# Two layers of causal convolution and GeGLU on one core: a new order of chunks and layers, with handover visits in halves

## The chip, the cores and the metric

The kernel runs on one core of one Trainium2 chip. The metric is device time in microseconds (us): the median of 3 runs of the kernel before is 909.96 us (909.64 to 910.38). One execution was profiled; its span is counted from the first to the last instruction of the program.

The core's engines run side by side, each through its own list of instructions in order: PE (matrix products; its weight loads are listed as PEld), DVE and ACT (elementwise work), POOL (small elementwise work and transfers), SP (transfers only). They wait for each other through semaphores. DMA transfers are issued by SP, POOL or ACT and carried out by 16 DMA engines.

## The reference

`x` has 2048 tokens of 576 features (bf16 inputs). Two times over, a convolution layer A and a feed-forward layer B are added to it:

```python
x = A_q
for _ in range(2):
    h = layernorm(x)
    k4 = sum(shift(A_k, 3 - t) * A_shift_k[:, t] for t in range(4))   # causal, 4 taps
    kv = k4 * A_v
    y = causal_conv(kv, A_ssm_k) + kv * A_ssm_D                       # 2048 taps, by FFT
    x = x + h * y
    h = layernorm(x)
    x = x + (gelu(h @ B_w_gate) * (h @ B_w_up)) @ B_w_down            # 576 -> 4608 -> 576
```

`y` doesn't depend on `x`, so one convolution serves both layers.

## The kernel before

**Chunks, units, passes, visits.** The tokens are cut into 4 chunks of 512, each of 4 rows of 128 tokens. A unit is (layer, chunk); units 0 to 7 are (0,0) (0,1) (1,0) (1,1) (0,2) (0,3) (1,2) (1,3). The feed-forward weights don't stay on the chip: a pass streams all of them once, in 3 phases of 12 feature tiles (of 128 features), and serves the units in its list, `passes = [[0], [1, 2], [3, 4], [5, 6], [7]]`. One phase of one unit is a visit; there are 24.

**A visit** (the loop at L1640 and after). For each of 12 feature tiles `gu` (L1099 to L1104) does 18 matmuls of 64x128 weights by 512 tokens, in pairs on the two halves of the array's rows, into one of three PSUM banks in turn; ACT makes the GELU (L1691 or L1700; L1692 copies the other factor too when ACT has time) and DVE the product into `hT` (L1693, L1701), which frees the bank. Then `two_rows` (L1755) does the product with the down weights for rows 0 and 1, then 2 and 3: 48 matmuls of 288 columns a row, in two steps, first half of the array's rows, then the other half. Between the steps stands `hold` (L1135): a NOP on ACT or DVE that waits for the first step and that PE waits for before the second. DVE adds the result to `x_c` (L1798 to L1806).

**The handover chain.** When the last phase of a layer-0 unit ends, each row of its chunk goes: sum into `x_c` with the row's sum (DVE L1798), mean (POOL L933), sum of squares (ACT L941), `rstd` (POOL L948, L949), `yh` = 1 + y * rstd (ACT L977), `x_c` * ... (DVE L987), mean, squares and `rstd` again, normed row `xn` (DVE L1016, L1018), and its transpose into `xnT` by DMA (`spread`, L1055: two DMA transposes from SP, of 5 and of 4 blocks of 128 columns). `xnT` is what the next unit's feature tiles read.

**The convolution** works in 4 blocks of 512 tokens. For block m the spectra of block and filter are made on PE (`fwd`, `fwd_h` for block 1, 8 matmuls at a step; `fwd4` with `quarter` for blocks 2 and 3, 4 matmuls at a step, whose sums and differences DVE finishes), the spectra of all earlier blocks are multiplied on DVE (`prod`), folded, and turned back on PE (`inverse`). This work is spread between the feature tiles.

**What sets the order.** The program is written out instruction by instruction in Python. `Pace` keeps a planned clock of PE, DVE and ACT with costs such as `C_GU` for a feature tile; `fill` (L1165) puts other work behind each tile until a limit. `weights` (L1145) issues weight loads from SP: 3 buffers of gate and up weights (`load_wgu`, L868, three transfers each, 4 feature tiles) and 3 of down weights (`load_wd`, L880). A load waits in SP's queue until PE has left the buffer, and what stands behind it waits too.

Of the kernel before, what the change touches and what calls it, by code (L numbers as in the profile page):

```python
# [24 lines left out]
NP = 3  # L25
# [8 lines left out]
C_P0, C_P1, C_AC = 1.28, 1.35, 0.7  # L34
C_TT, C_ST, C_BN, C_NORM, C_HT, C_GELU, C_EVA, C_EVD, C_YH = 0.74, 0.80, 0.47, 0.62, 0.615, 0.51, 0.56, 0.72, 0.7
C_HB = 0.345
C_FOLD = 0.46
# [3 lines left out]
SLOW, PRESS = 5.0, 22.0  # L41
# [93 lines left out]
class Conv:  # L135
# [9 lines left out]
    def __init__(self, tc, ctx, pace, gwork, xtp, A_k, A_v, A_shift_k, A_ssm_k, A_ssm_D, ident, cps, ypool):  # L145
# [22 lines left out]
        self.nT = self.cst.tile([P, 5, P], BF16, name="nT")  # L168
        self.V_ = self.cst.tile([P, 2, RT, P], BF16, name="V")
        self.nV = self.cst.tile([P, 3, P], BF16, name="nV")  # L170
# [124 lines left out]
    def fwd_eo(self, src, kt, s, h, ring, scale=1.0):  # L295

        nc = self.nc
        ps = yield from self.both_steps(lambda ps: [ps[:, e, 0:HW] for e in range(2)],
                                   [([self.fw(kt, s, i + e) for e in range(2)],
                                     [src(i + e)[:, h * HW:(h + 1) * HW] for e in range(2)]) for i in (0, 2)])  # L300
        eo = self.eo_tile(ring)
        nc.scalar.activation(out=eo[:], in_=ps[:, :, 0:HW], func=ACT.Copy, scale=scale)
        return eo

# [16 lines left out]
    def quarter(self, src, e, s, h, scale=1.0):  # L321
# [5 lines left out]
        eo = self.eop.tile([P, 2, HW], F32, tag="eo", name="eo")  # L327
        nc.scalar.activation(out=eo[:], in_=ps[:, :, 0:HW], func=ACT.Copy, scale=scale)  # L328
        return eo

    def cross(self, eo, lo, hi):
        for dst, op in ((lo, ALU.add), (hi, ALU.subtract)):
            self.nc.vector.tensor_tensor(out=dst, in0=eo[:, 0, :], in1=eo[:, 1, :], op=op)

# [59 lines left out]
    def step(self, m, kv=None, loaded=False):  # L394
# [74 lines left out]
        def fwd(kt, s, h):  # L469
            def run():  # L470
                if s == 0 and h == 0:
                    for k in (kt, kt + 2):
                        kc[k] = self.kcp.tile([P, 2, D], BF16, tag="kc", name="kc")
                free, ring = self.eo_free(True)
                self.eo_at[ring].popleft()
                cur = self.cur
                eo = yield from self.fwd_eo(lambda i: self.vt_[m][:, i, :], kt, s, h, ring)
                done = t.on_act(C_EVA, max(t.pe + 0.25 + LAG, free))
                self.ps_free[cur] = done
                if (kt, s, h) == (1, 1, 1):  # L480
                    self.fwd_at[m] = t.pe + 0.25
                cols = slice(h * HW, (h + 1) * HW)

                def fin():
                    self.cross(eo, kc[kt][:, s, cols], kc[kt + 2][:, s, cols])
                    when = t.on_dve(2 * C_BF, done + LAG)
                    self.eo_at[ring].append(when + LAG)
                    mark(("kc", kt, s, h), when + LAG)
                    if s == 1 and h == 1 and m < self.NB - 1:
                        for k in (kt, kt + 2):  # L490
                            self.spill(self.Kd[m][k], kc[k], when + LAG)
                self.U.append((done + LAG, 2 * C_BF, fin))
            return run

        hh = self.hh if m == 1 else {}

        def fwd_h(kt, s, h):
            def run():
                if (kt, s, h) == (0, 0, 0):
                    self.hh_tiles()  # L500
                free, ring = self.eo_free(True)
                self.eo_at[ring].popleft()
                cur = self.cur
                eo = yield from self.fwd_eo(self.ht[m], kt, s, h, ring, 1.0 / NFQ)
                done = t.on_act(C_EVA, max(t.pe + 0.25 + LAG, free))
                self.ps_free[cur] = done
                if (kt, s, h) == (1, 1, 1):
                    self.hf_at[m] = t.pe + 0.25
                    if loaded:
                        self.hr_free[0] = self.hr_free[1] = self.hf_at[m]  # L510
                cols = slice(h * HW, (h + 1) * HW)

                def fin():
                    self.cross(eo, hh[kt][:, s, cols], hh[kt + 2][:, s, cols])
                    when = t.on_dve(2 * C_BF, done + LAG)
                    self.eo_at[ring].append(when + LAG)
                    mark(("hh", kt, s, h), when + LAG)
                    if s == 1 and h == 1:
                        for k in (kt, kt + 2):
                            self.spill(self.Hd[m][k], hh[k], when + LAG)  # L520
                        if kt == 1:
                            self.hd_at[m] = when + 10.0
                self.U.append((done + LAG, 2 * C_BF, fin))
            return run
# [3 lines left out]
        def v(kt, a, part):  # L528
            def run():
                K = kc[kt] if a == m else kr[(kt, a)][1]  # L530
                if m == 1 and a == 0:
                    prs[part, a, kt] = self.prod(part, K, hh[kt], hr[(kt, a)][1][:, part, :])
                else:
                    prs[part, a, kt] = self.prod(part, K, hr[(kt, a)][1])

                def fin(when):
                    if part == 1:
                        if m == 1:
                            self.hr_free[hr[(kt, a)][0]] = when if a else NEVER
                        else:  # L540
                            self.hr_free[hr[(kt, a)][0]] = when
                        if a < m:
                            self.kr_free[kr[(kt, a)][0]] = when
                return fin
            return run

        def more(kt, part, a):
            def run():
                if a == 1:
                    acc[kt, part] = self.acp.tile([P, D], F32, tag="ac", name="ac")  # L550
                into = acc[kt, part][:]
                nc.vector.tensor_tensor(out=into, in0=prs[part, 0, kt] if a == 1 else into, in1=prs[part, a, kt], op=ALU.add)

                def fin(when):
                    if m == 1 and part == 1:
                        self.hr_free[hr[(kt, 0)][0]] = when
                return fin
            return run
# [40 lines left out]
        for kt in KTS:  # L599
            order = [(a, part) for a in range(m + 1) for part in range(2)]  # L600
            if m == 1:
                order = order[2:]
                for k in (kt, kt + 2) if kt < 2 else ():
                    for part in range(2):
                        self.V.append((get(("ld", k, 0), ("ldk", k), *[("hh", kt, s, h) for s in range(2) for h in range(2)]),
                                       C_P1 if part else C_P0, v(k, 0, part)))
            for a, part in order if kt < 2 else sorted(order, key=lambda k: k[1]):
                keys = [("ld", kt, a)] + ([("kc", kt % 2, s, h) for s in range(2) for h in range(2)] if a == m or m > 1 else [])
                self.V.append((get(*keys), C_P1 if part else C_P0, v(kt, a, part)))
                if a > 0:  # L610
                    self.V.append((now, C_AC, more(kt, part, a)))
                if kt >= 2 and a == m:
                    self.V.append((now, 2 * C_EVD, both(kt, part)))
                    self.V.append((now, 2 * C_TB, shift(kt - 2, part)))
# [5 lines left out]
        def fwd4(filt, e, s, h):  # L620
# [3 lines left out]
            def run():  # L624
                free = self.eo_at["eo"].popleft()
                cur = self.cur
                eo = yield from self.quarter(src, e, s, h, scale)
                done = t.on_act(C_EVA, max(t.pe + 0.13 + LAG, free))
                self.ps_free[cur] = done
                if last:  # L630
                    (self.hf_at if filt else self.fwd_at)[m] = t.pe + 0.13
                cols = slice(h * HW, (h + 1) * HW)

                def first():
# [4 lines left out]
                    else:  # L639
                        if s == 0 and h == 0:  # L640
# [4 lines left out]
                    self.eo_at["eo"].append(t.on_dve(2 * C_BF, done + LAG) + LAG)  # L645

                def second(n):
                    def run():
# [9 lines left out]
                        if n == 1 and last:  # L658
# [7 lines left out]
                            if filt:  # L666
                                self.hd_at[m] = when + 10.0
                    return run
# [1201 lines left out]
```

## Time and profile before

| | us |
|---|---|
| median of 3 runs | 909.96 |
| span of the profiled execution | 907.9 |
| difference | 2.06 |
| PE busy | 902.9 |
| DVE busy | 556.8 |
| ACT busy | 364.5 |
| POOL busy | 142.0 |

The page gives busy time by engine, the span in 40 slices, the chain of work that ended last, and groups of instructions by line with their count and mean duration. A matmul's listed duration reaches from its start to its modelled end, and matmuls overlap; how fast PE goes is read from the starts of successive groups. DMA issues are listed with the time from issue to landing.

### The profile page before, as it was taken

How to read it: one execution, taken by the hardware profiler on the slowest of the kernel's cores; microseconds unless marked ns; L12 is line 12 of the kernel's file. 1: busy time of each engine (PE TensorE's matmuls, PEld its weight loads, DVE VectorE, ACT ScalarE, POOL GpSimd, SP SyncE). 2: the span in 40 equal slices, each digit the busy share in tenths (PEclk: the TensorE clock that was granted, in tenths of full speed). 3: DMA queues.
4: the chain of work that ended last, by engine and by line, in shares of the span. 5: the costliest groups of instructions: out<-in, count | busy, mean ns of one | idle time of the engine just before them, and what ended most of it. 6: DMA issues, size and time to landing. Idle time of an engine off the chain costs nothing.

```text
span 907.9 us, 24267 instructions
## 1 busy us (share of the span) xinstructions
PE 902.9 (99%) x10465; PEld 601.3 (66%) x10465; DVE 556.8 (61%) x1109; ACT 364.5 (40%) x677; POOL 142.0 (16%) x311
## 2 busy tenths in 40 slices
PE   9999999999999999999999999999999999999998
PEld 7757656577576675775766766757757657667666
DVE  8898988654789876667888744553333334433332
ACT  7784446625434356354244233451121224321211
POOL 5423003320113012230023001220000002100000
PEclk9999999999999999999999999999999999999999
DMA  9999967877519503974934702762720820777630
GB/s 242 314 265 285 231 143 137 179 232 135 170 56 258 128 3 67 270 201 102 251 120 123 167 14 69 138 124 63 136 79 3 157 80 14 142 178 179 135 102 28
DMA packets 128272, 129.73 MB, mean 143 GB/s; under 512 B 43298, under 2 KB 120483, under 8 KB 128164
## 3 DMA queue, kind: packets, MB, share of 16 engines
q1 hardware_dynamic: 119138, 93.22, 47.7%
q0 software_dynamic: 8880, 34.36, 11.0%
q8 instruction: 82, 1.34, 0.6%
q10 hardware_dynamic: 146, 0.59, 0.2%
q14 instruction: 26, 0.21, 0.1%
HBM read 106.91 MB, written 11.80 MB: 131 GB/s over the span
## 4 chain that ended last, share of the span: by engine, by line
PE 98%; POOL 0%; ACT 0%; issue 0%; DVE 0%; ACTq 0%
PE gu L1103 61%; PE dn L1768 30%; PE cps L310 2%; PE ps L284 2%; PE dn L1729 1%; PE ps L1344 0%; PE ps L1103 0%; PE ps L1479 0%; POOL rstd L1564 0%; PE ps L1257 0%; PE ps L1315 0%; PE cps L373 0%; PE ps L278 0%; ACT yh L1526 0%; PE ps L1373 0%
## 5 line engine op out<-in xcount | busy, mean ns | idle before, releaser
L1103 PE MATMUL gu<-xnT,wgu 64*128 64x512 bf16 x5148 | 561.4, 376 | 0.0
L1103 PEld LDWEIGHTS <-wgu 64*128 64x128 bf16 x5220 | 293.2, 94 | 260.6 <-issue 0.7
L1768 PE MATMUL dn<-wd,hT 64*128 64x288 bf16 x4512 | 293.9, 283 | 0.0
L1768 PEld LDWEIGHTS <-hT 64*128 64x128 bf16 x4512 | 254.4, 94 | 26.2
L1700 ACT ACTIVATE ga<-gu 128x512 f32<-128x512 f32 x175 | 104.4, 597 | 311.0 <-PE gu L1103 307.8
L1701 DVE TENSOR_TENSOR hT<-ga,gu 128x512 bf16<-128x512 f32 x175 | 120.1, 687 | 167.5 <-ACT ga L1700 167.3
L1691 ACT ACTIVATE ga<-gu 128x512 bf16<-128x512 f32 x111 | 66.2, 597 | 149.9 <-PE gu L1103 143.9
L1693 DVE TENSOR_TENSOR hT<-ga 128x512 bf16<-128x512 bf16 x112 | 47.0, 421 | 59.6 <-ACT ga L1692 59.5
L1692 ACT CAST ga<-gu 128x512 bf16<-128x512 f32 x111 | 64.3, 579 | 0.0
L933 POOL TENSOR_SCALAR means<-s 128x1 f32<-128x1 f32 x28 | 10.4, 372 | 248.7 <-DVE x_c L1798 219.4
L1804 DVE SCALAR_TENSOR_TENSOR x_c<-dn,means,x_c 128x576 f32<-128x576 f32 x28 | 22.8, 815 | 28.4 <-PE dn L1768 28.4
L1806 DVE TENSOR_TENSOR x_c<-x_c,dn 128x576 f32<-128x576 f32 x32 | 24.1, 752 | 25.8 <-PE dn L1768 25.5
L949 POOL TENSOR_TENSOR rstd<-ve,neghalf_t 128x1 f32<-128x1 f32 x56 | 35.4, 632 | 4.7
L345 DVE TENSOR_TENSOR prod<-prod 128x576 bf16<-128x576 bf16 x64 | 29.3, 458 | 2.2
L328 ACT ACTIVATE eo<-cps 128x576 f32<-128x576 f32 x32 | 20.8, 651 | 23.5 <-PE cps L310 17.3
L1785 DVE TENSOR_TENSOR xn<-x_c,dn 128x576 bf16<-128x576 f32 x15 | 11.3, 754 | 26.5 <-PE dn L1768 24.2
L656 DVE TENSOR_TENSOR kc<-ab,cd 128x288 bf16<-128x288 f32 x64 | 25.3, 452 | 0.0
L443 POOL DMA_DIRECT2D kr<-Kd x20 | 11.2, 558 | 88.2 <-DVE prod L344 88.2
L941 ACT ACTIVATE junk<-x_c,nm 128x576 bf16<-128x576 f32 x28 | 21.5, 769 | 2.2 <-POOL nm L933 1.6
L977 ACT ACTIVATE yh<-y,rstd 128x576 f32<-128x576 bf16 x28 | 21.4, 768 | 1.1 <-POOL rstd L949 1.1
L448 POOL DMA_DIRECT2D hr<-Hd x32 | 17.8, 556 | 24.1 <-DVE prod L344 22.6
L948 POOL TENSOR_SCALAR ve<-ss 128x1 f32<-128x1 f32 x56 | 13.9, 248 | 43.7 <-ACT junk L941 43.4
(177 smaller groups left out, 626.4 us busy)
## 6 DMA issues: line engine op xcount, KB each, us to landing
wgu<-in_B_w_gate_dram SPq DMA_DIRECT2D x45, 576.0 KB, 5.9
wd<-in_B_w_down_dram SPq DMA_DIRECT2D x30, 864.0 KB, 7.1
wgu<-in_B_w_up_dram SPq DMA_DIRECT2D x45, 512.0 KB, 7.5
hr<-Hd POOLq DMA_DIRECT2D x32, 288.0 KB, 4.6
kr<-Kd POOLq DMA_DIRECT2D x24, 288.0 KB, 3.9
Kd<-kc POOLq DMA_DIRECT2D x12, 288.0 KB, 6.4
k<-in_A_k_dram POOLq DMA_DIRECT2D x3, 1008.0 KB, 10.3
wgu<-in_B_w_up_dram SPq DMA_DIRECT2D x45, 64.0 KB, 7.3
```

The source lines that it names most:

```text
L345: nc.vector.tensor_tensor(out=dst[:, cols], in0=pr[:, 0, cols], in1=pr[:, 1, cols], op=ALU.subtract if part == 0 else ALU.add)
L656: nc.vector.tensor_tensor(out=into[k][:, plane, cols], in0=a, in1=b, op=op)
L949: nc.gpsimd.tensor_tensor(out=v["rstd"][:], in0=ve[:], in1=neghalf_t[:, 0:1], op=ALU.pow)
L1103: nc.tensor.matmul(cols(pair[:, s, :]), lhsT=w[r0:r0 + HK, k, gi * P:(gi + 1) * P], rhs=cols(xnT[r0:r0 + HK, blk_of[k], :]), start=(k == 0 ...
L1691: nc.scalar.activation(out=ga[:, 0, :], in_=pair[:, 0, :], func=ACT.Gelu_apprx_tanh)
L1692: nc.scalar.copy(out=ga[:, 1, :], in_=pair[:, 1, :])
L1693: nc.vector.tensor_tensor(out=hT[:, fi, :], in0=ga[:, 0, :], in1=ga[:, 1, :], op=ALU.mult)
L1700: nc.scalar.activation(out=ga[:], in_=pair[:, 0, :], func=ACT.Gelu_apprx_tanh)
L1701: nc.vector.tensor_tensor(out=hT[:, fi, :], in0=ga[:], in1=pair[:, 1, :], op=ALU.mult)
L1768: nc.tensor.matmul(acc[:, g, 0:HW], lhsT=lhs[r], rhs=wn[r, g * HW:(g + 1) * HW], start=step == 0 and fi == 0, stop=step == 1 and fi == FP - 1)
L1804: nc.vector.scalar_tensor_tensor(out=xh, in0=acc[:, :, 0:HW], scalar=m_[:, 0:1], in1=xh, op0=op, op1=ALU.add)
L1806: nc.vector.tensor_tensor(out=xh, in0=xh, in1=acc[:, :, 0:HW], op=ALU.add)
```

## The change

1. `passes = [[0], [2], [1], [3, 4], [5, 6], [7]]`: chunk 0 goes through layer 0 and straight through layer 1, then chunk 1. There are 6 passes over the weights in place of 5, still 24 visits.
2. Unit 2 now follows unit 0 and unit 3 follows unit 1 with no visit between. The last visit of units 0 and 1 and the first of units 2 and 3 (`SPLIT`) are done in halves: 12 feature tiles for the 256 tokens of rows 0 and 1, those rows' down products, then the same for rows 2 and 3. So the first half of the next unit needs rows 0 and 1 alone.
3. For units 2 and 3 (`at_once`) a row's 5-block transpose is issued by SP and its 4-block transpose by ACT; rows are normed two at a time.
4. Weight loads in these visits get due times by halves (`pieces`, `size`).
5. Block 1 of the convolution takes the form of blocks 2 and 3 (`fwd4`, `quarter`); products are multiplied first and joined after.
6. Small ones: a scratch row `junk` of its own, `nT` and `nV` in the start's memory, `prep` of chunk 1 later, costs of `Pace` retuned.

```diff
-    passes = [[0], [1, 2], [3, 4], [5, 6], [7]]
+    passes = [[0], [2], [1], [3, 4], [5, 6], [7]]
     NWB = len(passes) * NP
+    at_once = [units.index((1, c)) for c in range(2)]
+    SPLIT = {(units.index((0, c)), NP - 1) for c in range(2)} | {(n, 0) for n in at_once}
...
         tasks = [gate_step(c, j, g, v[j], layer == 1)]
+        if ui in at_once:
+            return tasks + [norm(i) for i in range(j - 1, j + 1) if j % 2]
...
-    def spread(xnT, j, xn):
+    def spread(xnT, j, xn, engs):
         tok = slice(j * P, (j + 1) * P)
         for (b0, nb, c0) in ((0, 5, 0), (5, 4, HK)):
-            nc.sync.dma_start_transpose(out=xnT[:, b0:b0 + nb, tok], in_=xn[:, c0:c0 + nb * P])
+            engs[b0 // 5].dma_start_transpose(out=xnT[:, b0:b0 + nb, tok], in_=xn[:, c0:c0 + nb * P])
...
-            spread(xnT_of[ui], j, xn)
+            if ui in at_once:
+                spread(xnT_of[ui], j, xn, (nc.sync, nc.scalar))
+                t.on_act(C_ISSUE)
+            else:
+                spread(xnT_of[ui], j, xn, (nc.sync, nc.sync))
             xn_done[ui] = j + 1
...
-            if conv_first:
+            if conv_first and not pressing():
...
         def steps(filt, ready):
-            limit = lambda: max(ready(), 0.0 if self.eo_at["eo"] else NEVER)
-            if m > 1:
-                for h in range(2):
-                    for e in range(2):
-                        for s in range(2):
-                            self.Pq.append((limit, 0.25, fwd4(filt, e, s, h)))
-                return
-            for kt in range(2):
-                for s in range(2):
-                    for h in range(2):
-                        self.Pq.append((lambda: max(
-                            ready(), 0.0 if self.eo_at["eo"] or self.eo_at["yh"] else NEVER), 0.49, (fwd_h if filt else fwd)(kt, s, h)))
+            limit = lambda: max(ready(), 0.0 if self.eo_at["eo"] or m == 1 and self.eo_at["yh"] else NEVER)
+            for h in range(2):
+                for e in range(2):
+                    for s in range(2):
+                        self.Pq.append((limit, 0.25, fwd4(filt, e, s, h)))
...
+            split = (ui, ph) in SPLIT
+            def inputs(rows):
+                coming[0], due_at[0] = ui, t.pe
+                while xn_done.get(ui, 0) < rows:
...
+            inputs(RT // 2 if split else RT)
...
+            def features(part=None):
+                last = final and part != 0
+                size = 1.0 if part is None else 0.5
+                cols = (lambda a: a) if part is None else (lambda a: a[:, part * CH // 2:(part + 1) * CH // 2])
+                while late:
+                    add_late()
+                for fi in range(FP):
...
+                        gu(pair, w, gi, cols, xnT)
...
+                    if gi == FG - 1 and last:
+                        group = fi // FG * FG * C_GU
+                        when_due(t.pe + ((FP - FG) * C_GU + 12.0) * size + group * (pieces(at + 1) - size), load_wgu, n + 3)
...
+            for part in range(2) if split else (None,):
+                if part == 1:
+                    inputs(RT)
...
+                features(part)
+                ahead[:] = [t.pe + RT * FP * C_DN, None if split or at + 1 == len(visits) else visits[at + 1][2]]
+                for j in (0, 2) if part is None else (2 * part,):
+                    rows(j)
```

More of the change, by code (lines that the diff above doesn't have):

```diff
@@ L467, in step @@
                            load(kt, a)))
[L469 to L493, printed above, removed]
@@ L495, in step @@
-        hh = self.hh if m == 1 else {}
[L497 to L524, printed above, removed]
@@ new lines, in step, with products, mult, run @@
+        acc = {}
+        halfway = set()
+        def products(kt, items):
+            tiles = {}
+            own = m == 1 and items[0][0] == 0
+            def mult(n):
+                a, part = items[n]
+                def run():
+                    if not tiles:
+                        for i in range(len(items)):
+                            tiles[i] = self.prp.tile([P, 2, D], BF16, tag="prod", name="prod")
+                    K = kc[kt] if a == m else kr[(kt, a)][1]
+                    self.mul(part, K, hh[kt] if own else hr[(kt, a)][1], tiles[n])
+                    def fin(when):
+                        if (kt, a) not in halfway:
+                            halfway.add((kt, a))
+                            return
+                        self.hr_free[hr[(kt, a)][0]] = NEVER if own else when
@@ L542, in fin, with join @@
                         if a < m:
                             self.kr_free[kr[(kt, a)][0]] = when
-                return fin
-            return run
+                    return fin
+                return run
+            def join():
+                for n in reversed(range(len(items))):
+                    a, part = items[n]
+                    dst = hr[(kt, a)][1][:, part, :] if own else tiles[len(items) - 1][:, n, :]
+                    self.join(part, tiles[n], dst)
+                    prs[part, a, kt] = dst
+                return lambda when: None
@@ L547, in more, with ready @@
+            def ready(a):
+                if own:
+                    return get(("ld", kt, 0), ("ldk", kt), *[("hh", kt % 2, s, h) for s in range(2) for h in range(2)])
+                return get(("ld", kt, a), *([("kc", kt % 2, s, h) for s in range(2) for h in range(2)] if a == m or m > 1 else []))
+            steps = [(ready(items[n][0]), C_M1 if items[n][1] else C_M0, mult(n)) for n in reversed(range(len(items)))]
+            return steps, (now, len(items) * C_BF + 0.02, join)
         def more(kt, part, a):
@@ new lines, in ssm_geglu_kernel, with begin @@
+            inputs(RT // 2 if split else RT)
+            if xn_done[ui] < RT:
+                due_at[0] = t.pe + FP * C_GU / 2 + 2 * FP * C_DN
+            else:
+                due_at[0] = t.pe + FP * C_GU + RT * FP * C_DN
+                coming[0] = next((v[2] for v in visits[at + 1:] if v[2] != ui), None)
+            def begin():
+                for kind, n in at_start.get((ui, ph), []):
+                    if kind == "es":
+                        act_early(n)
+                    elif kind == "x":
+                        load_x(n)
+                    else:
+                        for j in range(RT):
+                            vq.extend(prep(n, j))
@@ L1755, in two_rows @@
                 some = math.ceil((gone[-1] + 0.5 - t.pe) * 2 / C_DN) - (FP - 1)
-                some = max(0, min(FP - 3, some)) if j == 0 else 0
+                some = max(0, min(FP - 3, some)) if j == 0 or split else 0
                 order = ([(0, 0, fi) for fi in range(FP - 2)] + [(1, 0, fi) for fi in range(some)] +
```

256 lines of the change are left out of this document (126 added, 130 removed).

## The prediction

> **What bounds the kernel now.** I read the page's busy times and slices first, then the chain of work that ended last, then the stretches.
>
> ```profile
> span 907.9 us, 24267 instructions
> PE 902.9 (99%) x10465; PEld 601.3 (66%) x10465; DVE 556.8 (61%) x1109; ACT 364.5 (40%) x677; POOL 142.0 (16%) x311
> PE 98%; POOL 0%; ACT 0%; issue 0%; DVE 0%; ACTq 0%
> ...
> 446.82 23.31 PE gu L1103 x216
> 470.13 11.76 PE dn L1768 x192
> 481.89 23.31 PE gu L1103 x216
> ...
> 40.00:435.00 395.00, 394.90 (x4640) 259.37 (x4640) 304.22 (x644) 199.27 (x379) 78.12 (x167) 1.00 0.69 170
> ```
>
> PE sets the end: 98% of the chain is PE. A busy PE could hide stalls, so the starts matter: a visit takes 23.31 + 11.76 = 35.07 us, which is 216 matmuls of 512 columns at 107.9 ns and 192 of 288 columns at 61.25 ns, and one visit follows the other without a gap. From 40 to 435 us, where convolution and handovers lie, PE is idle for 0.10 us. So no waiting is there to be won: the change can gain only what it takes out of PE's own work, and any wait that it puts in front of PE is lost in full.
>
> **PE's own work.** Counted in the two kernels' lists of instructions: block 1's spectra fall from 128 matmuls of 288 columns to 64; 864 matmuls of 512 columns become 1728 of 256; nothing else changes on PE.
>
> ```profile
> 40.02 3.12 PE L1103 MATMUL ps<-xnT,wgu 64*128 64x256 bf16 x54
> 42.98 0.41 PE L310 MATMUL cps<-ht,T 64*128 64x288 bf16 x4
> ...
> 44.21 0.65 PE L310 MATMUL cps<-ht,T 64*128 64x288 bf16 x8
> 44.70 2.11 PE L1103 MATMUL gu<-xnT,wgu 64*128 64x512 bf16 x18
> ```
>
> Eight spectra matmuls move the next start by 0.49 us, 61.25 ns each: 64 fewer give -3.9 us. The 54 matmuls of 256 columns take 42.98 - 40.02 = 2.96 us, 54.8 ns each: 1728 x 54.8 - 864 x 107.9 = 94.7 - 93.2 = +1.5 us (0 if they took half of a full one, +4.4 at 56.5 ns, the listed end of that group). Together **-2.4 us** (-3.9 to +0.5).
>
> **The sixth pass over the weights** costs no PE time: slices that moved 230 to 314 GB/s ran with PE at 9 tenths.
>
> ```profile
> PE   9999999999999999999999999999999999999998
> GB/s 242 314 265 285 231 143 137 179 232 135 170 56 258 128 3 67 270 201 102 251 120 123 167 14 69 138 124 63 136 79 3 157 80 14 142 178 179 135 102 28
> ...
> q1 hardware_dynamic: 119138, 93.22, 47.7%
> ```
>
> A single-unit pass of 3 x 35.07 = 105 us moves at most 93.22 / 5 = 18.6 MB (q1 has little but weights), 178 GB/s. In a split visit a weight buffer is released with tile 3 of the second half and wanted again at the half's end, 17.7 - 4 x 0.99 = 13.7 us later, against some 8 us to load it (both below). Each us by which a load outgrew that would be lost in full; I take 0.
>
> **The handovers.** Four times PE now needs two rows' transposes before it may go on: H1 and H2 (rows 0, 1 and rows 2, 3 of unit 2), H3 and H4 (of unit 3). The cover is half a visit: 12 x 18 x 54.8 ns + 96 x 61.25 ns = 11.8 + 5.9 = 17.7 us, in which the whole chain of two rows must run. The prices:
>
> ```profile
> L1700 ACT ACTIVATE ga<-gu 128x512 f32<-128x512 f32 x175 | 104.4, 597 | 311.0 <-PE gu L1103 307.8
> L1692 ACT CAST ga<-gu 128x512 bf16<-128x512 f32 x111 | 64.3, 579 | 0.0
> L941 ACT ACTIVATE junk<-x_c,nm 128x576 bf16<-128x576 f32 x28 | 21.5, 769 | 2.2 <-POOL nm L933 1.6
> L977 ACT ACTIVATE yh<-y,rstd 128x576 f32<-128x576 bf16 x28 | 21.4, 768 | 1.1 <-POOL rstd L949 1.1
> L1693 DVE TENSOR_TENSOR hT<-ga 128x512 bf16<-128x512 bf16 x112 | 47.0, 421 | 59.6 <-ACT ga L1692 59.5
> L1016 DVE TENSOR_SCALAR xn<-x_c,nm,rstd 128x576 bf16<-128x576 f32 x28 | 16.1, 576 | 1.5 <-POOL rstd L949 1.5
> L1018 DVE COPY xn<-xn 128x64 bf16<-128x64 bf16 x28 | 5.1, 182 | 1.0
> L700 ACT ACTIVATE y<-cps 128x576 bf16<-128x576 f32 x12 | 7.6, 655 | 11.0 <-PE cps L310 11.0
> ...
> L1058 SPq DMA_TRANSPOSE xnT<-xn x56: 1200/1257/2270, 142.2 to 786.1; - x56
> DMA to landing us min/median/max: 2.5/2.6/5.2
> ...
> wgu<-in_B_w_up_dram SPq DMA_DIRECT2D x45, 512.0 KB, 7.5
> ...
> 126.10 0.60 SPq L874 DMA_DIRECT2D wgu<-in_B_w_gate_dram  x1
> 126.76 0.63 SPq L875 DMA_DIRECT2D wgu<-in_B_w_up_dram  x1
> 127.44 0.63 SPq L876 DMA_DIRECT2D wgu<-in_B_w_up_dram  x1
> ```
>
> One queue issues a transpose every 1.26 us, each lands 2.6 us after its issue began: four from SP alone would take 3 x 1.26 + 2.6 = 6.4 us. In the changed program the two queues don't run side by side: wherever the queue changes, the transpose waits for the other queue's to have landed. H1 reads ACT row 0, then SP row 0 (waits for it), ACT row 1 (waits), SP row 1 (waits): four landings in a row, 4 x 2.6 = 10.4 us. H2: both of SP, then both of ACT; H3: both of ACT, then both of SP; H4: SP, ACT, ACT, SP.
>
> The Trainium skill ("DMA: Bandwidth & Descriptors", section "Silent corruption: two transposing streams in flight at once") asks for just this: transposes from SP and from ACT are two streams, and the later one's first must wait for the earlier one's full completion count. No run here shows what happens without.
>
> Times from the start of each half, with a 256-column GELU at 0.4 us (an estimate between half of 597 ns and all of it), the copy likewise, and 0.2 us from PE to ACT (the x8 group's listed end, 0.65, is 0.16 us past the next start):
>
> H1. ACT has its first transpose behind GELU and copy of tile 10 of 0 to 11, whose matmuls end at 10.85; ACT also does four sums of squares and two `yh`, 6 x 0.77 = 4.6 us, which by the order of its list pushes it by some 0.3: 12.1. Landings at 14.7, 17.4, 20.1; the fourth can be issued at 20.2. But SP's queue holds three weight transfers between its two transposes (16.1 to 17.9, 1.9 us of issue); the large second one lands 7.5 us after its issue at 16.7, so at 24.2, and the fourth transpose, behind it, at 24.6 (22.8 if it lands alone; 25.4 at the 5.2 us row). Loss 24.6 - 17.7 = **6.9**. Behind ACT's second transpose stands the `hold` NOP for which PE waits between the down steps: PE stops from 15.0 to 18.8 and ends at 21.7, so even early landings leave 4.0.
>
> H2. Four inverse steps (4 full matmuls, 0.49 us each) and a spectrum step (0.25) lengthen the cover to 19.9. Both `xn` stand on DVE behind tile 11's `hT`: 11.8 + 0.2 + 0.4 + 0.4 + 0.2 = 13.0, done at 14.6; SP's second is issued at 15.05 and lands at 17.7, ACT's go at 17.7 and 18.95, landing at 21.6. Behind them on ACT stand a `hold` NOP and a PSUM eviction (0.66 us) that PE needs, from 18.95 + 1.26 = 20.2 to 20.9, and some 20 matmuls of PE's after that (1.3 us): PE ends near 22.2. Loss **2.3** (1.6 to 4).
>
> H3. ACT's second is behind row 1's `xn` (13.9), lands at 16.6; SP goes at 16.7 and 17.95, landing at 20.6, or 21.0 behind the weights issued from 11.9. Loss **3.3** (2.2 to 5). H4. Cover 18.2; landings 14.3, then ACT from 15.6 to 18.2, then 20.9. Loss **2.7** (2 to 4.5). Unit 4, prepared in the second half of unit 3's visit, has its last norm behind ACT's work after tile 11 and lands at 19.3 against 18.4: **0.9** (0 to 2).
>
> Sum of losses 16.1 us, bounds 4.0 + 1.6 + 2.2 + 2.0 = 9.8 and (H1 at 9, two landings at the maximum) 24.5.
>
> **The sum.** 907.9 - 2.4 + 16.1 = 921.6 of span. The median stands 909.96 - 907.9 = 2.06 us above the span, work outside the first and last instruction, unchanged: **923.7 us**.
>
> **The rivals.**
>
> *The queues overlap, or landings come early enough (faster).* Place: the waits between SP's and ACT's transposes. If they cost nothing, the last transposes land at about 15, 18, 17 and 17 us, inside 17.7 to 19.9 us of cover, and only the -2.4 stays: 907.9 - 2.4 + 2.06 = 907.5. It decides where a pair of rows has landed 17.7 us after its half began. Against it stand the waits in the program and 2.6 us as the least that each change of queue costs; for it that both lists leave PE saturated elsewhere. 0.08. With losses of 1 to 4 us left it would be within 0.2% (1.8 us either way, about what a measurement of this kernel can tell from no change): 0.04.
>
> *PE runs slow after the new gaps.* PE has no gap like these before, except at the start:
>
> ```profile
> 3.88 2.20 PE ps L1315 x8
> ...
> 28.05 3.20 PE ps L1479 x26
> ...
> 4.00:7.00 3.00, 3.00 (x20) 1.75 (x19) 2.31 (x4) 2.33 (x5) 0.01 (x1) 1.00 0.96 316
> ```
>
> Of the same 128x288 form, 8 took 275 ns each at 3.88 us, 26 took 123 ns each at 28.05 us, though the granted clock is shown as 1.00. If the first 5 us after a gap run at half rate, a gap costs 2.5 us more. H1 has two gaps of 3 us or more, H3 one, H2 and H4 shorter ones: two gaps hit give 923.7 + 5 = 928.7, all five 936. 0.20. The Trainium skill ("TensorE: Matmul & The Clock Gate", "Part 1: The HAM clock gate") has PE fall to half rate after an idle window of about 3.4 us and stay there for about as long; by that figure a gap costs an estimated 1.7 us, and gaps under the window nothing. No gap of that length stands in this trace.
>
> *Everything at its earliest (less slow).* At the lower bounds 907.9 - 2.4 + 9.8 + 2.06 = 917.4; that is the low end of the forecast's case, not one of its own.
>
> **How the numbers follow.** Forecast, slower through waiting transposes with PE at full rate (916 to 931): 0.68. Slower with a slow PE besides (925 to 936): 0.20. Faster 0.08, same 0.04. So slower 0.88. The range from 915 to 932 leaves out the 0.12 of the faster cases and some 0.08 of the slow-PE case above it.
>
> **What would show it.** In the changed kernel's trace PE should be idle some 16 us in all between about 125 and 420 us, in four places, the largest ahead of unit 2's first tile, each ended by a transpose's landing, or by ACT's NOP behind a transpose. SP and ACT transposes should never be in flight together, each 2.5 us or more after the other. Half tiles should start every 0.99 us. Wrong would be: gaps ended by DVE, POOL or weights; landings well under 2.5 us; PE idle under 5 us; or a total below 912.

## The result, and the profile after

The changed kernel takes **968.54 us** (median of 4 runs, 966.54 to 969.51) where the kernel before takes 909.86 us on the same chip: ratio 1.0642, 95% interval 1.0627 to 1.0657. The forecast was 923.7 us, 915 to 932. The direction was right; the loss is 58.7 us where 13.7 were forecast. The profiled execution took 966.54 us, its span is 964.8 us, 56.9 us longer than before.

The page of the changed kernel, PE's rows, the granted clock, and the shares of the chain that ended last:

```profile
PE 915.9 (95%) x11265; PEld 608.8 (63%) x11265; DVE 568.7 (59%) x1191; ACT 371.3 (38%) x748; POOL 142.6 (15%) x311
PE   9999994999899999677899999999999999999998
PEclk9999997999899999889999999999999999999999
PE 88%; DMA 6%; DVE 3%; issue 1%; ACT 1%; POOL 1%; SPq 0%; ACTq 0%; DVEq 0%; POOLq 0%
```

PE is no longer busy throughout: there is a hole in slice 6 (145 to 169 us), a small one in slice 10 (241 to 265 us) and a long one in slices 16 to 19 (386 to 482 us), and in slices 6, 10, 16 and 17 the clock is below full speed, which it nowhere was before. DMA has come into the chain with 6%. What PE waited for in the changed kernel (us in total, times, longest):

```profile
PE gu L1086 <- DMA xnT<-xn: 21.6, 4, 13.3
PE dn L1775 <- ACTq L1118: 10.0, 3, 8.4
PE gu L1086 <- issue: 4.9, 2, 4.5
PE cps L300 <- ACT eo L318: 2.2, 1, 2.2
PE gu L1086 <- DMA wgu<-in_B_w_up_dram: 2.1, 1, 2.1
PE gu L1086 <- DMA wgu<-in_B_w_gate_dram: 1.7, 1, 1.7
```

The first two lines are the forecast's mechanism: the transposes into `xnT`, and `hold`'s NOP (L1118) that stands behind a transpose in ACT's list. Most of the third, 4.5 us, is the second stop at H1: no releaser is listed, but PE goes on at 166.85 us, 0.09 us after the last transpose landed. The fourth is the first stop at H4, for a PSUM eviction of ACT's (L318, at 434.13 us) that stands behind ACT's two transposes. The last two are weights, which the forecast had at nothing. The chain of waits of the changed kernel through H1 and H3 shows what a transpose took (start, us, what):

```profile
145.15 7.78 DMA xnT<-xn
...
153.07 2.61 DMA xnT<-xn
...
157.01 0.02 ACTq L1118
...
162.34 4.51 issue
166.85 5.15 PE gu L1086 x47
...
396.33 13.55 DMA xnT<-xn
...
411.35 2.59 DMA xnT<-xn
...
414.07 5.97 PE gu L1086 x75
```

The order is the forecast's: ACT, then SP once ACT's has landed, then ACT again. But ACT's took 7.78 us at H1 and 13.55 us at H3 where the forecast had 2.6. SP's list in the changed kernel shows what was in flight: weight loads issued within 4 us ahead of the transposes of 145.15 and 396.33 us.

```profile
141.82 0.59 SPq L853 DMA_DIRECT2D wgu<-in_B_w_gate_dram  x1
142.46 0.64 SPq L854 DMA_DIRECT2D wgu<-in_B_w_up_dram  x1
...
394.51 0.60 SPq L853 DMA_DIRECT2D wgu<-in_B_w_gate_dram  x1
395.31 0.60 SPq L854 DMA_DIRECT2D wgu<-in_B_w_up_dram  x1
```

At H2 nothing else was in flight, and the same four transposes (line L1037 from 180 to 195 us) landed as forecast:

```profile
DMA to landing us min/median/max: 2.4/2.5/2.6
```

Stretches of the changed kernel (us, then the busy time and count of PE, PEld, DVE, ACT, POOL, then the granted clock):

```profile
148.37:157.07 8.70, 0.29 (x6) 0.09 (x1) 2.94 (x7) 0.00 (x0) 0.00 (x0) 0.67 0.70 110
157.07:161.50 4.43, 4.43 (x38) 3.29 (x39) 0.77 (x2) 0.00 (x0) 0.22 (x1) 0.50 1.14 215
162.05:166.85 4.80, 0.29 (x6) 0.03 (x1) 0.77 (x2) 0.00 (x0) 0.21 (x1) 0.80 0.43 64
166.85:171.80 4.95, 4.95 (x48) 4.08 (x50) 0.70 (x2) 1.79 (x5) 0.76 (x2) 0.50 0.55 178
188.00:190.00 2.00, 0.55 (x11) 0.32 (x7) 1.71 (x4) 0.23 (x1) 0.00 (x0) 1.00 0.51 102
252.00:257.00 5.00, 4.97 (x26) 2.03 (x28) 0.00 (x0) 0.92 (x2) 0.00 (x0) 0.50 1.15 214
400.46:414.07 13.61, 0.29 (x6) 0.03 (x1) 0.77 (x2) 0.87 (x2) 1.00 (x4) 0.62 0.83 210
414.07:417.00 2.93, 2.93 (x28) 2.34 (x30) 0.37 (x1) 0.38 (x1) 0.00 (x0) 0.50 0.89 296
436.10:441.80 5.70, 0.37 (x7) 0.16 (x3) 1.55 (x3) 1.66 (x3) 0.22 (x1) 0.97 0.76 77
```

The stretches of 8.70, 4.80, 13.61 and 5.70 us are gaps. The stretches right behind the first three have a clock of 0.50: PE is listed as fully busy and does half the work. So has 252 to 257 us, behind two waits for weights of 1.9 and 2.4 us with one matmul between them. The gap of 1.7 us inside 188 to 190 us leaves the clock at 1.00.

Taking every start of a matmul against the start before it plus that matmul's own time (107.9, 54.8 or 61.25 ns), the 56.9 us are:

| | forecast | measured |
|---|---|---|
| PE's own work | -2.4 | -2.0 |
| H1, idle | 6.9 | 8.6 + 4.7 = 13.4 |
| H2 | 2.3 | 1.7 |
| H3 | 3.3 | 13.5 |
| H4 | 2.7 | 2.5 + 5.6 = 8.0 |
| unit 4 | 0.9 | 2.4 + 1.1 = 3.5 |
| unit 2's third phase (weights) | 0 | 1.9 + 2.4 = 4.3 |
| three more gaps under 1 us each | 0 | 2.0 |
| matmuls at half speed behind six of these places | 0 | 11.2 |
| delays of under half a us | 0 | 1.3 |
| sum | 13.7 | 56.9 |

The weights' stall lies ahead of the visit that starts at 249.5 us; it is unit 2's third phase, though the expectations below call it the second. PE's own work: unit 0's second visit starts at 79.3 us in place of 83.05 (-3.8), and later visits have 1.8 us more.

### The profile page after: what moved, and what is told of

Same layout as the page of the kernel before. It is cut to its first block, busy times and chain, and to the rows that moved or that the text cites. A ratio compares the mean times of both kernels' runs of the same rounds, so it can differ in the third digit from the quotient of the medians.

```text
span 964.8 us, 26089 instructions
## 1 busy us (share of the span) xinstructions
PE 915.9 (95%) x11265; PEld 608.8 (63%) x11265; DVE 568.7 (59%) x1191; ACT 371.3 (38%) x748; POOL 142.6 (15%) x311
## 4 chain that ended last, share of the span: by engine, by line
PE 88%; DMA 6%; DVE 3%; issue 1%; ACT 1%; POOL 1%; SPq 0%; ACTq 0%; DVEq 0%; POOLq 0%
PE gu L1086 58%; PE dn L1775 24%; DMA xnT<-xn 4%; DMA wgu<-in_B_w_up_dram 2%; PE ps L284 1%; PE cps L300 1%; PE dn L1736 1%; DVE x_c L1811 1%; PE ps L1329 0%; DVE kc L636 0%; PE ps L1464 0%; PE ps L1086 0%; DVE prod L331 0%; PE ps L1240 0%; POOL rstd L1548 0%
## 5 line engine op out<-in xcount | busy, mean ns | idle before, releaser
L1086 PE MATMUL gu<-xnT,wgu 64*128 64x512 bf16 (+1 forms) x6012 | 576.9, 349 | 31.8 <-DMA xnT<-xn 21.6
L1086 PEld LDWEIGHTS <-wgu 64*128 64x128 bf16 x6084 | 321.9, 95 | 276.6 <-issue 31.1
L1775 PEld LDWEIGHTS <-hT 64*128 64x128 bf16 x4512 | 239.0, 94 | 55.0 <-issue 11.5
L1708 DVE TENSOR_TENSOR hT<-ga,gu 128x512 bf16<-128x512 f32 (+1 forms) x198 | 122.9, 623 | 196.1 <-ACT ga L1707 195.9
L1707 ACT ACTIVATE ga<-gu 128x512 f32<-128x512 f32 (+1 forms) x198 | 107.7, 545 | 299.3 <-PE gu L1086 297.4
L1698 ACT ACTIVATE ga<-gu 128x512 bf16<-128x512 f32 (+1 forms) x136 | 70.8, 520 | 170.7 <-PE gu L1086 166.3
L1700 DVE TENSOR_TENSOR hT<-ga 128x512 bf16<-128x512 bf16 (+1 forms) x137 | 50.4, 372 | 69.6 <-ACT ga L1699 69.3
L1699 ACT CAST ga<-gu 128x512 bf16<-128x512 f32 (+1 forms) x136 | 68.3, 503 | 0.0
L318 ACT ACTIVATE eo<-cps 128x576 f32<-128x576 f32 x48 | 30.9, 655 | 34.7 <-PE cps L300 28.2
L1792 DVE TENSOR_TENSOR xn<-x_c,dn 128x576 bf16<-128x576 f32 x15 | 11.3, 753 | 23.0 <-PE dn L1775 20.7
L1805 DVE SCALAR_TENSOR_TENSOR x_c<-dn,x_c 128x576 f32<-128x576 f32 x16 | 12.1, 757 | 20.0 <-PE dn L1775 19.2
L323 DVE TENSOR_TENSOR ab<-eo 128x288 f32<-128x288 f32 x48 | 19.3, 451 | 7.7 <-ACT eo L318 4.4
## 6 DMA issues: line engine op xcount, KB each, us to landing
k<-in_A_k_dram POOLq DMA_DIRECT2D x3, 1008.0 KB, 11.4
```

Of the source, the lines that this page charges most:

```text
L1086: nc.tensor.matmul(cols(pair[:, s, :]), lhsT=w[r0:r0 + HK, k, gi * P:(gi + 1) * P], rhs=cols(xnT[r0:r0 + HK, blk_of[k], :]), start=(k == 0 ...
L1698: nc.scalar.activation(out=cols(ga[:, 0, :]), in_=cols(pair[:, 0, :]), func=ACT.Gelu_apprx_tanh)
L1699: nc.scalar.copy(out=cols(ga[:, 1, :]), in_=cols(pair[:, 1, :]))
L1700: nc.vector.tensor_tensor(out=cols(hT[:, fi, :]), in0=cols(ga[:, 0, :]), in1=cols(ga[:, 1, :]), op=ALU.mult)
L1707: nc.scalar.activation(out=cols(ga[:]), in_=cols(pair[:, 0, :]), func=ACT.Gelu_apprx_tanh)
L1708: nc.vector.tensor_tensor(out=cols(hT[:, fi, :]), in0=cols(ga[:]), in1=cols(pair[:, 1, :]), op=ALU.mult)
```

## The experiments

The theory after the result: a DMA transpose lands only after the other transfers that are in flight, whichever queue issued them. So where weights (H1, H3) or POOL's `kr` and `hr` loads (H4) were moving, it took 6 to 14 us and not 2.6; the gaps that this made are long enough to halve PE's clock. Rivals: ACT's queue is slow by itself, the rows are normed late, or half speed comes from something other than the gap. A time without a range below is of one execution.

**The disputed duration by itself.** In the kernel before:

```diff
+            if ui in (6, 7):
+                for n in range(2 * j):
+                    (nc.sync if ui == 6 else nc.gpsimd).dma_start(out=conv.Hd[...], in_=conv.Hd[0][n % 4][:])
             spread(xnT_of[ui], j, xn)
```

> The kernel before; ahead of the two transposes of rows 0, 1, 2, 3 of units 6 and 7, where nothing else is in flight, stand 0, 2, 4 and 6 copies of 288 KB from one place in device memory to another, issued by SP itself for unit 6 and by POOL for unit 7. Theory A (a transpose lands behind what is in flight, on whichever queue): its landing, 2.5 to 2.6 us in this kernel before, grows with the number of copies, by some 1 us or more for each copy (POOL's loads of this size landed about 1.2 us apart in the changed kernel), so for 6 copies to 8 us or more, in both units. Rival H (only what stands ahead in the same queue delays it): it grows in unit 6 and stays at 2.6 us in unit 7. Rival J (only loads of weights delay it): it stays at 2.6 us in both. The total shows none of this, since these rows come a visit ahead of their use: 910 to 913 us; if landings were delayed past that slack, more.

It took 909.96 us beside 909.67, so the total was not disturbed. The transposes' line in this run: for unit 6 (copies from SP) rows 1, 2, 3, with 2, 4, 6 copies ahead:

```profile
DMA to landing us min/median/max: 2.6/3.3/4.0
...
DMA to landing us min/median/max: 4.2/4.6/5.0
...
DMA to landing us min/median/max: 6.3/6.8/7.3
```

In the kernel before, row 1's landed in 2.6 and 3.8 us and row 2's in 2.6 and 2.5, so the two copies added next to nothing and the four some 2 us. For unit 7 (copies from POOL), row 0 without copies, then the two transposes of row 2 (row 1 has weight loads beside it in both kernels):

```profile
L1058 SPq DMA_TRANSPOSE xnT<-xn x2: 1238/1244/1251, 768.6 to 769.8; - x2
DMA to landing us min/median/max: 2.5/2.5/2.6
...
L1058 SPq DMA_TRANSPOSE xnT<-xn x2: 1210/1280/1350, 782.3 to 783.5; - x2
DMA to landing us min/median/max: 5.8/9.0/12.1
```

POOL's list meanwhile:

```profile
781.63 5.16 POOL L1099 DMA_DIRECT2D Hd<-Hd  x10
```

Both rivals fall: from four copies on the landing grows, also when they are no weights and come from another engine's queue. POOL's case is the harder one. The transpose issued at 783.5 us landed 12.1 us later, at 795.7, though most of the ten copies were issued after it: the last of them, issued at 786.3, landed at 795.5. So from another queue even later transfers get ahead. The Trainium skill ("DMA: Bandwidth & Descriptors", section "Queues, rings and completion order") has each DMA engine serve the queues in turn, a packet at a time; that bears out that one queue's later transfers need not wait for another's earlier one, and it doesn't say that the transpose is the one that loses.

**No weights in flight.** In the changed kernel:

```diff
+        if n >= 9:
+            wgu[n] = wgu[n - 3]
+            return
...
+        if n >= 6:
+            wd[n] = wd[n - 3]
+            return
```

> The changed kernel, but from the second pass on no weights are loaded: the buffers keep the weights of the first pass, so the output of those passes is not the reference's. Theory A (a transpose lands only after every transfer that was in flight when it was issued): with no weight load in flight the transposes of H1 and H3 land 2.4 to 2.6 us after issue, as they did at H2; H4 keeps its 7 us landings behind POOL's kr and hr loads. Idle PE at H1, H2, H3, H4 then 4.0, 1.7, 3.3, 8.0 us in place of 14.0, 1.7, 13.5, 8.0, no idle time at unit 2's second phase, less time at a clock of 0.50: about 933 us (925 to 938). Theory B (the transposes issued by ACT land late by themselves, or the rows are normed late): the gaps at H1 and H3 stay, only the stall at unit 2's second phase and its slow clock go, 4.3 + 2.5 us: about 961 us.

941.19 us, between the two but nearer to theory A's 933 than to 961, and above its range. The transposes of H1 (140 to 155 us in this run), as far as their landings are recorded:

```profile
DMA to landing us min/median/max: 2.5/2.6/2.6
```

and the two longest of PE's waits, in total:

```profile
PE gu L1092 <- DMA xnT<-xn: 8.0, 2, 7.5
PE dn L1781 <- ACTq L1124: 6.0, 2, 4.5
```

H1 falls from 13.4 us idle to 2.9. The rest of the miss is H3, H4 and unit 4 (4.7, 10.3 and 3.7 us idle): ACT's transposes landed in 4.5 to 5.1 us behind POOL's spills of `kc` at H3, and in 9.3 to 10.4 us behind its `kr` and `hr` loads at H4, with no weight in flight. I had kept POOL's traffic for H4 only.

**All transposes from SP.**

```diff
-                spread(xnT_of[ui], j, xn, (nc.sync, nc.scalar))
-                t.on_act(C_ISSUE)
+                spread(xnT_of[ui], j, xn, (nc.sync, nc.sync))
```

> The changed kernel, but both transposes of every row come from SP; ACT issues none. Theory A (a transpose lands behind whatever is in flight, on whichever queue): the transposes still take 7 to 12 us beside weight loads, but they are in flight together, and ACT's hold NOP no longer stands behind one: H1 idle 14.0 to about 6, H3 13.5 to about 10, H4 8.0 to about 6, one slow-clock stretch less: about 951 us (944 to 960). Theory B (ACT's queue is what is slow): all land in 2.6 us, issued 1.25 us apart, and the four handovers lose 8 us together: 925 to 930 us.

961.43 us: 7 us better than the change, slightly above A's range and far from B's 925 to 930. In this run PE's waits are

```profile
PE gu L1085 <- DMA xnT<-xn: 34.1, 7, 9.1
PE gu L1085 <- DMA wgu<-in_B_w_up_dram: 3.9, 2, 3.3
```

The NOP behind ACT's transpose is gone from the list and the landings take its place: at H1 they took 7.1 to 8.3 us, at H3 7.6 to 9.8. ACT's queue is not what is slow, and issuing from two queues was not what cost most. PE idles 9.4 us at H1 and 9.3 at H3, less than in the changed kernel, but 10.2 at H4 and 7.2 at unit 4, more than there; A had not foreseen these two.

**No DMA transposes at the handovers.**

```diff
+            if xn_made[0][0] in at_once:
+                if conv.ps_free[0] > t.pe or xn_made[0][3] > t.pe:
+                    return
+                turn_row(*xn_made.popleft())
+                continue
```

> The changed kernel, but the rows of units 2 and 3 are transposed on PE and copied out of PSUM, with no DMA between norm and next tile. Theory A: only the landings were late, so the idle time at H1 to H4 falls from 37.2 us to under 8, with it 7 us of slow clock; the transposes of 8 rows on PE cost about 5 us; the stalls at unit 2's second phase and at unit 4 (4.3 + 3.5 us idle, some 4 us slow clock) stay: 928 to 940 us. Rival C (the norms themselves come too late, the transposes only show it): idle time of 20 us or more stays: over 950 us.

934.54 us (931.39 to 936.36), ratio to before 1.0268, interval 1.0251 to 1.0286: as theory A has it. H1 to H4 have 4.3 us of idle time left in all, so the norms were ready; 34 of the 58.7 us were the landings and what they drew along, PE's work for turning the rows already taken off. The largest waits left are for the weights of unit 2's third phase and at unit 4:

```profile
PE gu L1091 <- DMA wgu<-in_B_w_up_dram: 5.6, 1, 5.6
PE gu L1091 <- DMA xnT<-xn: 5.3, 2, 4.9
```

**Units 1 and 4 turned on PE as well** (`in (1, 2, 3, 4)` in the edit above).

> As the run with the rows of units 2 and 3 turned on PE, and the rows of units 1 and 4 too: no DMA transpose is left before 500 us. Theory A: unit 4's start (5.1 + 1.0 us idle and about 1.2 us slow clock) is cured; if the transposes of unit 1 are also what holds up the weights for unit 2's second phase, that stall (7.1 us and about 1.4 us slow clock) goes too: 934.5 - 14.7 + 4 for 8 more rows on PE = about 924 us. Rival G (POOL's Hd, kr and hr transfers, some 3 MB at that time, hold the weights up): that stall stays, about 931 us.

925.54 us. The weights' stall is gone, so it was unit 1's transposes, mixed with POOL's transfers, that held those weights up. Beside POOL's transfers alone a load of 512 KB issued at 223.0 us still took 11.8 us. The run takes away both the transposes' place in SP's queue and their traffic, and doesn't say which of the two cost more. PE's waits, of which these are the largest and the one for weights:

```profile
PE gu L1091 <- DVE x_c L1816: 3.1, 2, 1.6
...
PE gu L1091 <- DMA wgu<-in_B_w_up_dram: 0.7, 2, 0.4
```

No gap is left that lowers the clock (1.000 over the span).

A row turned on PE costs its next product 0.61 us (a row's nine transposes at 145.50 us, the next matmul at 146.11), so 16 rows cost 9.8 us. That, idle time of 6.2 us in small gaps, 1.5 us for tiles of 256 columns, less 3.9 us of spectra, leave about 2 us of the 15.5 us over the kernel before, in delays under half a us each. So the new order in halves has its price even without late landings.

**Weights issued earlier** (turned on PE for units 2 and 3 only):

```diff
-            if due[0][0] > t.pe + (HOLD if near else SOON):
+            if due[0][0] > t.pe + (HOLD if near and coming[0] != 1 else SOON):
```

> As the run with the rows of units 2 and 3 turned on PE, but while unit 1 is the next unit weight loads may be issued 30 us ahead of their due time and not 14. If the stall at unit 2's second phase is only a load issued too late, behind unit 1's transposes in SP's queue, its 7.1 us and 1.4 us of slow clock go: about 926 us. If the transfers of that time are simply more than the DMA engines move, it stays: 933 to 936 us.

931.49 us, between the two expectations, but inside the 931.39 to 936.36 us of the four runs that it is compared with, so the total decides nothing. In the trace the wait for weights shrank from 5.8 to 4.5 us (a gap of 1.3 us ahead of it, for DVE's sum into `x_c`, is the same in both) and moved from the phase's first tiles to its last four. The loads of the first eight were issued as soon as their buffers were free, at 203.2 and 211.3 us; the last load was issued at 238.2 us, behind eight transposes, some of whose issues took 4 to 5 us in SP's queue. So a late issue is a part of the stall; how much of the rest is the place behind the transposes and how much the traffic stays open.

**What a gap does to the clock.** In the kernel before, nine visits of units 5 to 7:

```diff
+                        late_ops = {13: 6, 14: 7, 15: 8, 16: 9, 17: 10, 18: 11, 19: 13, 20: 16, 21: 22}.get(at, 0) if j + n == 3 else 0
...
+                        for _ in range(late_ops):
+                            nc.scalar.activation(out=xw[:], in_=x_c[c][:, 0, 0:CH], func=ACT.Copy)
+                        if late_ops:
+                            nc.scalar.keepalive_nop([nc.scalar.lower_ap(acc[:, :, 0:HW])])
...
```

> The kernel before with nine gaps put in front of PE, one in each of nine late visits, where no convolution and no handover lie: ahead of the last hold NOP ACT does 6, 7, 8, 9, 10, 11, 13, 16 and 22 copies of 128x512 of some 0.6 us, so that PE should wait about 0.7, 1.3, 1.9, 2.5, 3.1, 3.7, 4.9, 6.7 and 10.3 us, 35 us in all. Theory D (the granted clock falls to 0.50 once PE has been idle for some 3.4 us, and comes back 3 to 5 us after PE resumes): only the four longest gaps are followed by matmuls at half speed, 1.3 to 2.5 us each: 910 + 35 + 7.5 = about 952 us (948 to 957). Rival E (every gap costs in proportion to its length): slow matmuls after the short ones too, about 958 us. Rival F (the half speed after the handovers came from late operands, not from the gap): no slow matmuls, about 945 us.

961.66 us, 51.6 more than before. The gaps came out at 0.8, 3.0, 2.2, 2.8, 3.5, 4.2, 6.9, 7.4 and 11.4 us, 42.2 in all (7 us longer than planned, which puts the total above D's range). The four microseconds behind the gaps of 3.0, 2.8, 3.5, 6.9 and 11.4 us:

```profile
591.00:595.00 4.00, 3.91 (x48) 2.66 (x49) 2.92 (x8) 2.38 (x5) 1.79 (x5) 1.00 1.13 197
666.20:670.20 4.00, 4.00 (x48) 2.67 (x49) 0.82 (x1) 0.93 (x2) 0.00 (x0) 1.00 0.48 124
704.70:708.70 4.00, 4.00 (x36) 2.58 (x37) 0.76 (x1) 0.55 (x1) 0.00 (x0) 0.66 0.01 2
...
789.20:793.20 4.00, 4.00 (x30) 2.56 (x31) 3.01 (x8) 2.08 (x4) 1.89 (x6) 0.50 0.00 0
...
883.10:887.10 4.00, 4.00 (x32) 2.63 (x33) 0.82 (x1) 0.54 (x1) 0.00 (x0) 0.53 0.29 65
```

Up to 3.0 us the clock stays at 1.00 in this run and 48 matmuls run in 4 us; from 3.5 us on it is 0.50 to 0.66 and there are 30 to 36. The slow matmuls cost 1.6, 1.6, 2.6, 2.2 and 1.7 us, 9.7 together: 42.2 + 9.7 = 51.9, the whole difference. Theory D against its rivals holds: the size of the gap beyond 3.5 us doesn't matter much, and no late operand is needed. The Trainium skill ("TensorE: Matmul & The Clock Gate", "Part 1: The HAM clock gate") puts the idle window at about 3.4 us; this run agrees, with the step between 3.0 and 3.5 us.

That step is no least length of a gap, though. In the run without weights PE stood for 2.9 us from 147.5 us, and the matmuls behind it ran slow, at a cost of 1.7 us:

```profile
148.00:152.00 4.00, 1.59 (x16) 1.07 (x18) 1.96 (x5) 0.38 (x1) 0.00 (x0) 0.83 0.33 66
152.00:156.00 4.00, 4.00 (x54) 2.92 (x52) 3.07 (x8) 0.00 (x0) 0.22 (x1) 0.75 0.01 4
```

In the run with the old order (the last one here) a gap of 2.5 us did the same, at 1.6 us. In the clock records of all these traces the stretches of half clock last 3.41 us or a multiple of it (6.83, 10.24, 13.65, 17.07), but for those that the program's end cuts short, and within one run they begin whole multiples of 3.41 us apart, the five of the run with set gaps too. So what counts may be how much of such a stretch a gap fills; no run here moves one gap along that grid, so this is not shown.

**No halves** (turned on PE, `SPLIT = set()`).

> As the run with the rows of units 2 and 3 turned on PE, but no visit in halves: all four rows of a unit must be there before its first tile. What the halves are worth: without their cover of 17.7 us PE waits the whole chain of the last two rows, some 12 to 15 us for each of units 2 and 3 where it waited 2 to 4 us, and each gap is followed by some 2 us of slow clock; the 1.5 us for tiles of 256 columns and the split's own idle time come back: 934.5 + 2 x (13 + 2) - 6 = about 958 us (948 to 968). If the halves bought nothing: 935 us or less.

946.04 us, below the range of 948 to 968. Without halves PE idles 17.5 us ahead of the rows' transposes, mostly for DVE's norms, and pays the slow clock there:

```profile
L1107 PE MATMUL cps<-ident,xn 128*128 128x128 bf16 x72 | 8.6, 298 | 17.5 <-DVE xn L993 14.2
```

So the halves are worth some 11.5 us of that order (one run against a median of four that lie 5 us apart), less than the 23 expected.

**The old order with the rest of the change** (`passes` as before, `at_once` and `SPLIT` empty, chunk 1 prepared as before).

> The changed kernel with the old order of passes, no visit in halves and no handover with two queues: what is left of the change is block 1 of the convolution in the form of blocks 2 and 3 and the small items. If 64 spectra matmuls fewer of 61.25 ns are saved in full, 909.9 - 3.9 = 906.0 us (905.3 to 906.8). Rival: DVE's finishing of the sums and differences or the new costs of the planner give it back as stalls: 908 to 912 us.

909.84 us (12 runs, 909.65 to 914.03), ratio 1.0004, interval 0.9995 to 1.0013: no difference, neither 906 nor over 910. PE's second visit does start 3.7 us earlier (79.4 us), but unit 1 starts at 156.1 us where it started at 157.1. In this run's list

```profile
PE cps L1102 <- DVE xn L993: 0.8, 2, 0.6
```

three rows of unit 1 are turned on PE (27 transposes; none in the kernel before) and PE waits for their norms, which DVE does at 147.1 to 153.2 us, before at 141.4 to 146.4. At 0.61 us a row that is 1.8 us, with 1.2 us of waiting 3.0, somewhat more than the 2.7 us lost by then; at the next visit (192.8 us, before 192.7) nothing of the lead is left. The likely reason for the late norms is that the new form of block 1 brings DVE's work forward and unit 1's rows are behind it; no run takes DVE's part alone, so this is argued and not shown. The profiled execution took 914.03 us, the most of the twelve: a further gap of 2.5 us at 375 us and the slow matmuls behind it, 1.6 us, make up the 4.2 us by which it is above the median. No version here beats the kernel before.

## Why the prediction was wrong

*Bounds and mechanism: right.* PE had no wait to give, so every new wait cost in full. The gaps were where the forecast put them, ended by a transpose's landing or by ACT's NOP, but for ACT's eviction at H4; SP's and ACT's transposes never ran side by side; half tiles start every 0.99 us (216 matmuls in 11.86 us from 382.51). PE's own work came to -2.0 us against -2.4. One reading of its bounds is off: the listed end of the group at 40.02 us gives 3.12 / 54 = 57.8 ns a matmul and not 56.5, so the upper bound should have been +2.7; the term itself used 54.8 ns and stands.

*The step that failed: "Landings at 14.7, 17.4, 20.1", four landings of 2.6 us each.* I took 2.6 us from the kernel before, median of a row whose largest was 5.2, and used the 5.2 only as an upper end, without asking what it had met. It is in this line of the kernel before (389 to 402 us):

```profile
DMA to landing us min/median/max: 3.2/4.0/5.2
```

That transpose was issued at 392.1 us with seven of POOL's `kr` and `hr` loads in flight and landed at 397.3, after the last of them (396.2). Two larger transposes of the filter from device memory, issued at 36.2 and 62.3 us beside bulk transfers, took 9.7 and 13.5 us. So the trace of before held the sign. H1 to H4 stand where weight buffers are refilled by half visits and POOL loads spectra. I let weights delay only what stood behind them in SP's queue. Measured: 7.8 and 8.3 us for ACT's at H1, 11.3 and 13.6 at H3, 7.2 and 6.4 at H4, and 2.4 to 2.6 at H2 where nothing moved. H2 was therefore forecast within 0.6 us, and the other three were too small by 6.5, 10.2 and 5.3 us. The serial order of ACT and SP made it worse, since two such landings follow each other at H1.

*PE slow after gaps: a rival at 0.20 that came true.* Its price of 2.5 us for a gap was at the upper end (1.3 to 2.5 here, 1.6 to 2.6 in the run with set gaps). It was put apart from the forecast because no gap of that length stood in the trace of before; the gaps turned out long enough at six places, 11.2 us. The forecast's own H1, with stops of about 3.8 and 2.9 us, already stood at the edge.

*The sixth pass at nothing: wrong by 4.3 us idle and 2.5 us of half speed.* The cover that I named, 13.7 us from release to use, was for split visits; here it was wider, but the load for unit 2's third phase was issued at 233.8 us, behind six of unit 1's transposes in SP's queue, 15 us after PE had left the buffer (211.0 + 4 x 1.94 = 218.8). Then it took 16 us and not 8, beside two more transposes and eleven transfers of POOL's. I had checked the average rate (178 GB/s) and not what else was to move in those 20 us.

*Unit 4, 0.9 against 3.5,* is outside its bounds of 0 to 2 too. Its transposes landed in 2.5 to 4.0 us but were issued only to 463.1 us, after H4's delay; turning it on PE removed this wait.

The upper end of the range, 932, was the sum of these terms at the largest landing seen. It could not hold a landing three times as long.

## What to carry to other kernels

The duration of a small transfer in a profile is that of its surroundings: before moving it next to bulk loads, look for rows in which it ran beside some, and list what all queues will have in flight at its new place. Where PE is the bound and a chain must fit under a cover, a DMA on that chain is better replaced by the engine itself (0.61 us a row here, against 7 to 14) or kept clear of loads. Count a gap of some 2.5 us or more on PE with about 2 us of slow matmuls behind it, though here some gaps of up to 3.0 us cost none.

## What the hardware showed that I had not expected

- A transpose by DMA landed 2.5 us after its issue alone, 6.3 to 7.3 us behind six copies of 288 KB in its own queue, and 12.1 us with ten in POOL's queue, most of them issued after it.
- Loads next to transposes land late too: 512 KB of weights took 16.4 us to land at 235.6 us beside them and POOL's transfers, and 11.8 us at 223.0 us with every row of units 1 to 4 turned on PE, beside POOL's alone; the median in the kernel before is 7.5 us.
- The cost of a gap does not follow its length: with set gaps 3.0 us cost nothing, 3.5 us cost 1.6 and 11.4 us cost 1.7, and in the old order 2.5 us cost 1.6.
